# Beta's gate instructions at another place in a handwritten order of attention and GLU work

## The chip, the cores and the metric

The kernel runs on one core of one Trainium2 chip. The metric is device time in microseconds (us): how long the one core takes for one launch. The version before was timed three times: 264.73, 264.46 and 265.0 us, median 264.73 us.

## What is computed

Two branches read the same input `x` of 2048 tokens by 512 features, and a gate per token mixes them:

```
g = _sigmoid((x * gate_w).sum(-1, keepdims=True))
a = _A_ref(x, A_wq, A_wk, A_wv, A_wo, A_beta)
b = _B_ref(x, B_w_gate, B_w_up, B_w_down)
return g * a + (1 - g) * b
```

Branch B is a gated GLU: `gelu(x @ w_gate) * (x @ w_up)`, then `@ w_down`, with an inner width of 1792. Branch A is attention with 32 heads of width 16, in four segments of 512 tokens. In a segment the causal softmax attention `a_dot` is computed, and beside it a read `a_mem` from a running memory that the earlier segments filled; a gate per head, made from the 32 numbers of `beta`, mixes the two:

```
g = _sigmoid(beta).reshape(1, H, 1, 1)
...
o = g * a_mem + (1.0 - g) * a_dot
```

Everything here is about where the instructions stand that make the two factors `g` and `1 - g` of this last line.

## The kernel before

The work of all engines is cut into named tasks, each a short list of instructions for one engine. The string `ORDER` (lines 862 to 916) lists all tasks in one sequence, written out by hand. `schedule` (L134) reads it, and each engine receives its own tasks in that sequence and works through them strictly in order; `finalize` (L200) puts in the semaphore waits that the data need. A digit behind a task's name chooses one of four PSUM banks (psD, 128 x 512 in fp32) for a matmul task, and a letter chooses the engine of an eviction (`a` ScalarE, `d` VectorE, which the profile calls DVE). So a matmul task that gets a bank must wait until the task before it in that bank has been evicted.

Names in the order: `K0_1`, `Q1_2`, `V1_3b`, `G0_6` and `U0_7` are projections, the first number being the segment; K, Q, G and U tasks have four 128 x 512 matmuls (L449), V tasks four of 256 or 257 columns (L499). `Kev`, `Qev`, `Vev` and `Gev` evict them (L442 and L507 on ScalarE, L443 and L506 on DVE). `kpada` and `kpadb` (L488, DVE) write masked copies of K. `phk` and `phq` with `a`, `b` or `c` are the three steps of the feature map of the memory (L461 DVE, L463 ScalarE, L465 DVE). `st0_1B` computes a tile of attention scores in the four-bank buffer psX (L602), `exp0_1B` is its exponential on ScalarE (L609), `msk0_1B` multiplies its diagonal blocks by the causal mask on GpSimd (L615, called POOL in the profile). psX exists once, so `st`, `exp`, `st`, `exp` alternate. `pv0_1` (L644, 128 matmuls) multiplies the first two tiles' probabilities with V; it writes four banks in turn: 2 and 3 in its first half, 0 and 1 in its second half. `tp0_d01` and the three like it transpose its result on DVE (L530), and `pvp0_01` (L667 and L668) normalizes it and multiplies it by `gq`, the factor `1 - g`. That is the first attention tile that needs `gq`. The other factor, `gfull`, is first read in segment 1 (`ndp`, L558).

These tasks make the two factors, in `head_gates` (L761):

```
one("betab", DVE, 0.8, [I(lambda e, g=g: e.tensor_copy(
    betab[32 * g:32 * g + 32, :].rearrange("p (t j) -> p t j", j=2),
    ball[32 * g:32 * g + 32, :].rearrange("p (t g j) -> p g t j", g=4, j=2)[:, g]), ...
    for g in range(4)], bias=-150.0)
...
I(lambda e: e.activation(gq[:, :], betab[:], ACTF.Exp), ...
I(lambda e: e.activation(gfull[:, :], ball, ACTF.Exp, scale=-1.0), ...
```

`betab` (L764) is four copies on DVE, each of 32 partitions x 8 bf16, from `ball`, the 32 numbers of beta that the load `ld_beta` spread over all partitions of the buffer omem. `bexp` is two exponentials on ScalarE: L776 makes `gq` (128 x 8) and L777 `gfull` (128 x 32). `gqa` (L779, POOL) adds one to `gq`, `gqb` (L780, DVE) takes its reciprocal, `gfull` (L782, POOL) adds one to the other. No other task reads `betab`.

In the order before, `betab` stands on DVE behind `Vev1_0b` and ahead of `Gev0_1` and `kpada0_3`. `bexp` stands on ScalarE between `exp0_1A` (and the tiny `gr0`, L430) and `exp0_1B`. On POOL the sequence is `goa0 msk0_0A msk0_1A gqa msk0_1C msk0_1D gfull msk0_1B`. `gqb` stands on DVE behind `kpada1_0` and `gob0` (L434), ahead of `Qev1_3`.

Of the kernel before, what the change touches and what calls it, by code (L numbers as in the profile page):

```python
# [864 lines left out]
Kev0_3:a Q0_0:0 ld_wg0b Qev0_0:a Q0_1:3 st0_0A gwtr:2 Kev0_1:d gwev Q0_3:0 ld_wv ld_wg0 Qev0_1:d V0_1b:1 V0_3a:2 V0_3b:3 exp0_0A Qev0_3:d Vev0_3a:a  # L865
Vev0_1b:a st0_0B Vev0_3b:d kpada0_2 kpada0_1 V0_0b:0 V0_1a:2 V0_2a:1 Vev0_0b:d G0_6:3 Gev0_6:d Vev0_1a:d Vev0_2a:d exp0_0B st0_0C exp0_0C Q0_2:0
G0_2:3 V0_2b:2 ld_x1_2 ld_x1_1 ld_x1_3 ld_x1_0 ld_beta st0_0D Vev0_2b:a exp0_0D Gev0_2:d kpadb0_1 Qev0_2:d phka0_0 V1_2b:1 V0_0a:3 G1_6:2 V1_0b:0
Vev1_2b:d phka0_2 st0_0E Vev0_0a:d Vev1_0b:d betab G0_1:1 Gev1_6:a exp0_0E Gev0_1:d Q1_2:3 V1_3b:2 V1_3a:0 kpada0_3 Qev1_2:d Vev1_3a:d phkb0_2 phkc0_2
Vev1_3b:d st0_1A gz0 exp0_1A gr0 bexp Q1_0:1 V1_0a:3 G1_5:0 Vev1_0a:d Gev1_5:d st0_1B Q1_1:2 K1_0:3 exp0_1B phkb0_0 ld_wu1 ld_x2_0 G0_5:0 Qev1_0:d
kpadb0_3 vsh0_21 st0_1C exp0_1C Qev1_1:d ld_x2_1 ld_x2_3 ktr0_3 ld_wg1 Gev0_5:d V1_2a:1 K1_3:2 K1_1:0 vsh0_01 Vev1_2a:a vsh0_20 ld_x2_2 ktr0_2 vsh0_00  # L870
ld_wd1 st0_1D phkc0_0 Kev1_1:d kpada1_1 G0_4:1 G0_3:0 Gev0_4:d Kev1_0:d Gev0_3:d Kev1_3:a ld_wd0 ld_wu0 ktr0_1 ktr0_0 vsh1_20 ld_wo V1_1a:2 Vev1_1a:d
exp0_1D st0_2A exp0_2A msk0_0B msk0_0D msk0_0C kpada1_0 msk0_0E goa0 gob0 msk0_0A msk0_1A gqa gqb msk0_1C msk0_1D gfull msk0_1B G0_0:1 Q1_3:3 G1_1:0
Qev1_3:d phqa1_0 st0_2B Gev0_0:d Gev1_1:a pv0_1:2301 exp0_2B tp0_d01 tp0_d00 pvp0_01 Q2_0:3 Qev2_0:d tp0_d11 st0_2C K1_2:2 Kev1_2:d pvp0_00 tp0_d10
gelu0 G0_8:3 G0_13:1 gd0_13 G0_10:2 G0_11:0 G0_9:1 gd0_8 gd0_10 gd0_9 gd0_11 G0_12:3 G0_7:2 gd0_12 G1_2:1 U0_0:0 gd0_7 Gev1_2:d pvp0_11 h0_0 U0_13:3
U0_10:2 h0_10 Q2_1:1 Qev2_1:d exp0_2C st0_2D mz0:0 U0_7:2 U0_9:1 pvp0_10 h0_13 exp0_2D phqb1_0 st0_2E exp0_2E phka1_0 h0_7 mza0 h0_9 ota0_0 phqa1_2
kpadb1_0 G1_4:3 U0_1:2 h0_1 Gev1_4:a V1_1b:0 st0_3A G1_0:1 U0_5:3 Q2_2:2 exp0_3A Vev1_1b:a Gev1_0:a Qev2_2:a kpadb1_1 st0_3B exp0_3B U0_11:0 U0_4:1
U0_12:2 st0_3C phkb1_0 exp0_3C phqc1_0 kpada1_2 h0_4 h0_5 U0_6:1 U0_2:3 h0_11 h0_12 phqb1_2 h0_2 G1_3:0 Gev1_3:d h0_6 kpadb1_2 st0_3D phka1_2 U0_3:2
h0_3 U0_8:3 h0_8 Q2_3:0 Qev2_3:d exp0_3D phkb1_2 msk0_2A msk0_2B msk0_2C msk0_3A msk0_2E msk0_2D msk0_3C goc0 msk0_3B st1_0A msk0_3D pv0_3:1230
exp1_0A st1_0B exp1_0B tp0_d20 tp0_d21 pvp0_20 tp0_d30 ota0_1 pvp0_21 tp0_d31 kpada1_3 out0_1_0:1 out0_1_1 out0_1_2 V2_0a:2 Vev2_0a:d G1_9:3 V2_1b:0
Vev2_1b:d wev0_1:d st1_0C G1_8:2 G1_10:0 G1_11:1 gelu1 gd1_9 G1_7:3 gd1_8 gd1_10 gd1_7 gd1_11 G1_13:2 gd1_13 G1_12:0 gd1_12 phqc1_2 phkc1_0 mzq0  # L880
pvp0_31 pvp0_30 ota0_3 V2_0b:3 Vev2_0b:d ota0_2 V2_1a:1 Vev2_1a:d out0_0_0:2 out0_0_1 out0_0_2 nd1_0:0 ndp1_0 phkc1_2 exp1_0C st1_0D exp1_0D K2_0:3
# [63 lines left out]
```

## Time and profile before

| What | Value |
|---|---|
| median of three runs | 264.73 us |
| the profiled execution's own time | 265.0 us |
| its span, first to last instruction | 263.3 us |
| time outside the span, 265.0 - 263.3 | 1.7 us |
| granted TensorE clock, mean | 0.999 |
| busy: TensorE (PE) / DVE / ScalarE (ACT) / POOL | 258.8 / 199.5 / 203.2 / 98.5 us |
| `betab` L764 | 4 copies, 160 to 645 ns, from 22.6 to 24.6 us |
| `bexp` L776, L777 | 198 and 218 ns, at 27.3 and 27.4 us |
| `gqa` L779 and `gfull` L782 | 241 ns at 29.5 us and 337 ns at 37.7 us |
| `gqb` L780 | 168 ns at 37.9 us |

Times inside the profile count from the start of the span. A row of the timeline gives the start, the duration, the engine, the line and the operation, and in brackets how long the engine had been idle before it and what ended that. Rows of equal instructions that follow each other are merged; x4 says how many. Matmuls overlap: a 512-column matmul is shown as lasting 380 ns, while the next one starts about 216 ns after it. On DVE an instruction often starts 0.08 us before the one ahead of it has ended. In what follows such overlaps are kept as the rows show them.

### The profile page before, as it was taken

The numbers are of one execution on the slowest core, as the hardware profiler recorded it, in microseconds if no ns is written. First come the engines' busy times: TensorE is split into PE (matmuls) and PEld (weight loads), VectorE is DVE, ScalarE is ACT, GpSimd is POOL, SyncE is SP. The second block draws the span as 40 slices with busy tenths as digits, with TensorE's granted clock in tenths as the row PEclk, the third lists the DMA queues.
The fourth block names the chain that finished last, engine by engine and source line by source line (L and its number), as shares of the span: only waits on it lengthen the run. The fifth ranks groups of instructions, "written<-read, shape, count | busy, mean of one in ns | idle before, by whom it ended". The sixth has DMA issues, their size and how long they took to land.

```text
span 263.3 us, 6705 instructions
## 1 busy us (share of the span) xinstructions
PE 258.8 (98%) x2849; PEld 123.0 (47%) x2849; DVE 199.5 (76%) x412; ACT 203.2 (77%) x171; POOL 98.5 (37%) x163
## 2 busy tenths in 40 slices
PE   8999999999999999999999999999999999999995
PEld 7655445444354543544445445444444433444542
DVE  1559979284888686778958988976895973899873
ACT  1389779889988878898987898788788788777312
POOL 5008363024510465104806384156500377345300
PEclk9999999999999999999999999999999999999999
DMA  7974499400010211430002200022450000001412
GB/s 184 267 95 157 93 282 345 118 2 1 0 33 2 55 47 32 94 80 2 2 0 67 39 0 0 5 41 62 47 100 0 2 1 22 2 0 42 62 42 80
DMA packets 31990, 16.50 MB, mean 63 GB/s; under 512 B 21592, under 2 KB 31960, under 8 KB 31960
## 3 DMA queue, kind: packets, MB, share of 16 engines
q1 hardware_dynamic: 31272, 15.22, 25.6%
q10 hardware_dynamic: 688, 0.85, 0.9%
q8 instruction: 22, 0.36, 0.6%
q14 instruction: 8, 0.07, 0.1%
HBM read 7.87 MB, written 2.10 MB: 38 GB/s over the span
## 4 chain that ended last, share of the span: by engine, by line
PE 93%; DVE 4%; DMA 2%; issue 1%; SPq 0%; DVEq 0%
PE psD L449 46%; PE psD L735 19%; PE psX L602 9%; PE psD L644 6%; PE psD L749 5%; PE psD L499 4%; PE psD L477 2%; DMA wk<-in_A_wk_dram 2%; PE psD L547 1%; PE psD L577 1%; DVE betab L764 1%; DVE vnat L506 1%; DVE qT L443 0%; DVE phk L465 0%; DVE kD L488 0%
## 5 line engine op out<-in xcount | busy, mean ns | idle before, releaser
L609 ACT ACTIVATE pt<-psX 128x2048 bf16<-128x2048 f32 x72 | 135.1, 1877 | 29.0 <-PE psX L602 27.4
L615 POOL TENSOR_TENSOR pt<-pt,ctri 128x256 bf16<-128x256 bf16 x128 | 91.4, 724 | 129.8 <-ACT pt L609 125.4
L449 PE MATMUL psD<-xT,wu 128*128 128x512 bf16 x224 | 54.6, 380 | 0.0
L449 PE MATMUL psD<-xT,wg 128*128 128x512 bf16 x224 | 53.4, 380 | 0.0
L735 PE MATMUL psD<-wd,gb 128*128 128x512 bf16 x224 | 53.2, 380 | 0.0
L720 DVE TENSOR_TENSOR gb<-psD,gb 128x512 bf16<-128x512 f32 x56 | 37.2, 681 | 10.8 <-PE psD L449 10.8
L449 PEld LDWEIGHTS psD<-xT,wg 128*128 128x128 bf16 x224 | 20.9, 98 | 24.5 <-issue 1.3
L735 PEld LDWEIGHTS psD<-wd,gb 128*128 128x128 bf16 x224 | 20.7, 98 | 24.3 <-issue 2.1
L449 PEld LDWEIGHTS psD<-xT,wu 128*128 128x128 bf16 x224 | 20.2, 98 | 24.7 <-issue 2.6
L602 PE MATMUL psX<-qT,kD 32*128 32x192 bf16 (+7 forms) x512 | 28.6, 287 | 0.0
L530 DVE STREAM_TRANSPOSE tT<-psD 128x512 f32<-128x512 f32 x32 | 21.8, 702 | 5.1 <-PE psD L644 4.6
L443 DVE CAST gb<-psD 128x512 bf16<-128x512 f32 x20 | 13.6, 688 | 12.0 <-PE psD L449 11.9
L602 PEld LDWEIGHTS psX<-qT,kD 32*128 32x128 bf16 x512 | 8.2, 92 | 25.1 <-ACT pt L609 13.8
L499 PE MATMUL psD<-wv,xT 128*128 128x257 bf16 (+1 forms) x128 | 18.2, 273 | 0.3 <-DVE qT L443 0.3
L753 DVE SCALAR_TENSOR_TENSOR ost<-psD,gtok,wds 128x512 bf16<-128x512 f32 (+1 forms) x17 | 11.9, 711 | 7.7 <-PE psD L749 7.6
L668 DVE SCALAR_TENSOR_TENSOR ob<-tT,gq,rc 128x256 bf16<-128x256 f32 x32 | 16.7, 522 | 1.1
L703 ACT ACTIVATE gb<-psD 128x512 bf16<-128x512 f32 x28 | 15.0, 594 | 3.4 <-PE psD L449 3.3
L644 PE MATMUL psD<-pt,vsh 64*17 64x128 bf16 (+7 forms) x512 | 17.2, 283 | 0.0
L644 PE MATMUL psD<-pt,vnat 64*17 64x192 bf16 (+7 forms) x512 | 17.1, 283 | 0.0
L449 PE MATMUL psD<-xT,wq 128*128 128x512 bf16 x64 | 16.3, 380 | 0.1
L749 PE MATMUL psD<-wo,oT 128*128 128x512 bf16 (+1 forms) x68 | 16.1, 367 | 0.0
L499 PEld LDWEIGHTS psD<-wv,xT 128*128 128x128 bf16 x128 | 11.7, 97 | 7.2 <-issue 1.3
(81 smaller groups left out, 260.6 us busy)
## 6 DMA issues: line engine op xcount, KB each, us to landing
out_dram<-ost SPq DMA_DIRECT2D x15, 128.0 KB, 1.9
wu<-in_B_w_up_dram SPq DMA_DIRECT2D x2, 896.0 KB, 8.5
wd<-in_B_w_down_dram SPq DMA_DIRECT2D x2, 896.0 KB, 6.8
vsh<-vnat SPq DMA_DIRECT2D x16, 68.0 KB, 2.7
wg<-in_B_w_gate_dram SPq DMA_DIRECT2D x1, 896.0 KB, 5.5
wq<-in_A_wq_dram SPq DMA_DIRECT2D x2, 256.0 KB, 3.3
wv<-in_A_wv_dram SPq DMA_DIRECT2D x1, 512.0 KB, 4.2
wo<-in_A_wo_dram SPq DMA_DIRECT2D x1, 512.0 KB, 4.7
```

What stands on the lines that cost most here:

```text
L449: one(name, PE, n * T_MM, [I(lambda e, i=i: e.matmul(BK[sl.i][:, :], lhs(i), rhs(i), start=(i == 0), stop=(i == n - 1)), reads(i), [bk(sl) ...
L499: one(f"V{s}_{m}{'ab'[hf]}", PE, 2 * T_MM, [I(lambda e, i=i, sl=sl, a=a, z=z, xs=xs: e.matmul(BK[sl.i][:, 0:z - a], xs(i), wv[:, i, a:z], ...
L530: one(f"tp{name}", DVE, 0.605, [I(lambda e, sl=sl, ti=ti: e.transpose(tT[ti][:, :], BK[sl.i][:, :]), [bk(sl)], [("tT", ti)])], bias=bias)
L602: ins.append(I(lambda e, t=t, kb=kb, ncol=ncol, c0=c0, g=g: e.matmul(XALL[:, g * 512 + c0:g * 512 + c0 + ncol], kD[(4 * s + t) % R_KD][32 ...
L609: one(f"exp{s}_{name}", ACT, 2048 * 0.000833 + 0.05, [I(lambda e: e.activation(pt[slot][:, :, :], xin, ACTF.Exp, scale=ATT_SCALE), [("X",) ...
L615: ins.append(I(lambda e, mv=mv: e.tensor_tensor(mv, mv, cm, ALU.mult), [("pt", slot), ("causal",)], [("pt", slot)]))
L644: ins.append(I(lambda e, kb=kb, slot=slot, c0=c0, n=n, g=g, r0=r0, sl=banks[j], va=va: e.matmul(BK[sl.i][32 * g:32 * g + 17, 64 * kb:512], ...
L668: I(lambda e, ti=ti, ri=ri, t=t, j=j, dst=dst: e.scalar_tensor_tensor(out=dst, in0=t_rows(ti), scalar=gq[:, 2 * t + j:2 * t + j + 1], in1= ...
L703: t = one(f"gd{s}_{ft}", ACT, 0.485, [I(lambda e, gi=gi, f=f, sl=sl: e.activation(gb[gi][:, f, :], BK[sl.i][:, :], ACTF.Gelu_apprx_tanh), ...
L720: one(f"h{s}_{ft}", DVE, 0.605, [I(lambda e, sl=sl, gi=gi, f=f: e.tensor_tensor(gb[gi][:, f, :], BK[sl.i][:, :], gb[gi][:, f, :], ALU.mult ...
L735: mm.append(I(lambda e, fb=fb, gi=gi, f=f, q=q, sl=sl: e.matmul(BK[sl.i][:, :], gb[gi][:, f, q], wd[:, fb, :], start=(fb == 0), stop=(fb = ...
L749: one(f"wo{s}_{qt}{sfx}", PE, 4 * T_MM * w / 512, [I(lambda e, kb=kb, q=q, so=so, c=c, w=w: e.matmul(BK[so.i][:, 0:w], oT[:, kb, q], wo[:, ...
```

## The change

Only the order string changes; no instruction is added, removed or altered, and the sequences on PE and in the DMA queue of SyncE stay the same. Five moves, in the order's own words (the rest of the string is only wrapped differently):

```diff
-Vev1_2b:d phka0_2 st0_0E Vev0_0a:d Vev1_0b:d betab G0_1:1 Gev1_6:a
+Vev1_2b:d phka0_2 st0_0E Vev0_0a:d Vev1_0b:d G0_1:1 Gev1_6:a
...
-Vev1_3b:d st0_1A gz0 exp0_1A gr0 bexp Q1_0:1
+Vev1_3b:d st0_1A gz0 exp0_1A gr0 Q1_0:1
...
-ld_wd1 st0_1D phkc0_0 Kev1_1:d
+st0_1D phkc0_0 betab Kev1_1:d
...
-exp0_1D st0_2A exp0_2A msk0_0B ... gob0 msk0_0A msk0_1A gqa gqb msk0_1C msk0_1D gfull msk0_1B
+exp0_1D bexp st0_2A exp0_2A msk0_0B ... gob0 msk0_0A msk0_1A msk0_1C msk0_1D gqa gfull msk0_1B
...
-Qev1_3:d phqa1_0 st0_2B Gev0_0:d Gev1_1:a pv0_1:2301
+Qev1_3:d phqa1_0 st0_2B Gev0_0:d gqb Gev1_1:a pv0_1:2301
```

Engine by engine: on DVE, `betab` goes from ahead of `Gev0_1` to between `phkc0_0` and `Kev1_1`, past 14 instructions of evictions, `kpada0_3`, `kpadb0_3`, `phkc0_2` and `phkc0_0`; `gqb` goes from behind `gob0` to between `Gev0_0` and `tp0_d01`, past `Qev1_3`, `phqa1_0` and `Gev0_0`. On ScalarE, `bexp` goes from behind `gr0` to between `exp0_1D` and `exp0_2A`. On POOL, `gqa` goes from behind `msk0_1A` to behind `msk0_1D`, so that it now stands just ahead of `gfull` and `msk0_1B`.

More of the change, by code (lines that the diff above doesn't have):

```diff
@@ L867 @@
 G0_2:3 V0_2b:2 ld_x1_2 ld_x1_1 ld_x1_3 ld_x1_0 ld_beta st0_0D Vev0_2b:a exp0_0D Gev0_2:d kpadb0_1 Qev0_2:d phka0_0 V1_2b:1 V0_0a:3 G1_6:2 V1_0b:0
-Vev1_2b:d phka0_2 st0_0E Vev0_0a:d Vev1_0b:d betab G0_1:1 Gev1_6:a exp0_0E Gev0_1:d Q1_2:3 V1_3b:2 V1_3a:0 kpada0_3 Qev1_2:d Vev1_3a:d phkb0_2 phkc0_2
-Vev1_3b:d st0_1A gz0 exp0_1A gr0 bexp Q1_0:1 V1_0a:3 G1_5:0 Vev1_0a:d Gev1_5:d st0_1B Q1_1:2 K1_0:3 exp0_1B phkb0_0 ld_wu1 ld_x2_0 G0_5:0 Qev1_0:d
-kpadb0_3 vsh0_21 st0_1C exp0_1C Qev1_1:d ld_x2_1 ld_x2_3 ktr0_3 ld_wg1 Gev0_5:d V1_2a:1 K1_3:2 K1_1:0 vsh0_01 Vev1_2a:a vsh0_20 ld_x2_2 ktr0_2 vsh0_00
@@ L871 @@
[L871 to L878, printed above, removed]
+Vev1_2b:d phka0_2 st0_0E Vev0_0a:d Vev1_0b:d G0_1:1 Gev1_6:a exp0_0E Gev0_1:d Q1_2:3 V1_3b:2 V1_3a:0 kpada0_3 Qev1_2:d Vev1_3a:d phkb0_2 phkc0_2
@@ new lines @@
+Vev1_3b:d st0_1A gz0 exp0_1A gr0 Q1_0:1 V1_0a:3 G1_5:0 Vev1_0a:d Gev1_5:d st0_1B Q1_1:2 K1_0:3 exp0_1B phkb0_0 ld_wu1 ld_x2_0 G0_5:0 Qev1_0:d kpadb0_3
+vsh0_21 st0_1C exp0_1C Qev1_1:d ld_x2_1 ld_x2_3 ktr0_3 ld_wg1 Gev0_5:d V1_2a:1 K1_3:2 K1_1:0 vsh0_01 Vev1_2a:a vsh0_20 ld_x2_2 ktr0_2 vsh0_00 ld_wd1
+st0_1D phkc0_0 betab Kev1_1:d kpada1_1 G0_4:1 G0_3:0 Gev0_4:d Kev1_0:d Gev0_3:d Kev1_3:a ld_wd0 ld_wu0 ktr0_1 ktr0_0 vsh1_20 ld_wo V1_1a:2 Vev1_1a:d
+exp0_1D bexp st0_2A exp0_2A msk0_0B msk0_0D msk0_0C kpada1_0 msk0_0E goa0 gob0 msk0_0A msk0_1A msk0_1C msk0_1D gqa gfull msk0_1B G0_0:1 Q1_3:3 G1_1:0
@@ new lines @@
+Qev1_3:d phqa1_0 st0_2B Gev0_0:d gqb Gev1_1:a pv0_1:2301 exp0_2B tp0_d01 tp0_d00 pvp0_01 Q2_0:3 Qev2_0:d tp0_d11 st0_2C K1_2:2 Kev1_2:d pvp0_00
+tp0_d10 gelu0 G0_8:3 G0_13:1 gd0_13 G0_10:2 G0_11:0 G0_9:1 gd0_8 gd0_10 gd0_9 gd0_11 G0_12:3 G0_7:2 gd0_12 G1_2:1 U0_0:0 gd0_7 Gev1_2:d pvp0_11 h0_0
+U0_13:3 U0_10:2 h0_10 Q2_1:1 Qev2_1:d exp0_2C st0_2D mz0:0 U0_7:2 U0_9:1 pvp0_10 h0_13 exp0_2D phqb1_0 st0_2E exp0_2E phka1_0 h0_7 mza0 h0_9 ota0_0
+phqa1_2 kpadb1_0 G1_4:3 U0_1:2 h0_1 Gev1_4:a V1_1b:0 st0_3A G1_0:1 U0_5:3 Q2_2:2 exp0_3A Vev1_1b:a Gev1_0:a Qev2_2:a kpadb1_1 st0_3B exp0_3B U0_11:0
@@ L879 @@
+U0_4:1 U0_12:2 st0_3C phkb1_0 exp0_3C phqc1_0 kpada1_2 h0_4 h0_5 U0_6:1 U0_2:3 h0_11 h0_12 phqb1_2 h0_2 G1_3:0 Gev1_3:d h0_6 kpadb1_2 st0_3D phka1_2
+U0_3:2 h0_3 U0_8:3 h0_8 Q2_3:0 Qev2_3:d exp0_3D phkb1_2 msk0_2A msk0_2B msk0_2C msk0_3A msk0_2E msk0_2D msk0_3C goc0 msk0_3B st1_0A msk0_3D pv0_3:1230
 exp1_0A st1_0B exp1_0B tp0_d20 tp0_d21 pvp0_20 tp0_d30 ota0_1 pvp0_21 tp0_d31 kpada1_3 out0_1_0:1 out0_1_1 out0_1_2 V2_0a:2 Vev2_0a:d G1_9:3 V2_1b:0
```

## The prediction

> **What bounds the kernel.** I read the page first (busy times, chain), then the chain of waits in order of time, then the timeline of each engine around the moved instructions. The page's chain says that TensorE sets the end almost everywhere:
>
> ```profile
> PE 93%; DVE 4%; DMA 2%; issue 1%; SPq 0%; DVEq 0%
> ```
>
> So a saving counts only where PE waits. In the chain of waits (start, us, what) the 4% of DVE is one block:
>
> ```profile
> 22.64 0.06 DVE gzr L506
> 22.70 0.57 DVE betab L764
> ...
> 24.12 0.53 DVE betab L764
> ...
> 24.68 0.69 DVE gb L443
> ...
> 28.61 0.05 issue
> 28.66 2.76 PE psD L449 x12
> ...
> 39.98 2.19 PE psD L644 x108
> ...
> 72.62 2.08 PE psD L644 x126
> ```
>
> From 18.97 to 28.66 us the path runs through DVE, and `betab` is on it for 2.0 us. From 28.66 until 259.4 every piece is PE. The last two lines are for later: `pv0_1` takes 2.19 us, the same product in the next pair of tiles 2.08. Where PE really stood still is in its own timeline:
>
> ```profile
> 24.96 0.39 PE L602 MATMUL psX<-qT,kD 32*128 32x512 bf16 x4
> 25.42 1.04 PE L449 MATMUL psD<-xT,wq 128*128 128x512 bf16 x4
> 26.80 0.61 PE L499 MATMUL psD<-wv,xT 128*128 128x256 bf16 x4 [0.34 <-DVE qT L443]
> 27.25 1.02 PE L449 MATMUL psD<-xT,wg 128*128 128x512 bf16 x4
> 28.20 0.40 PE L602 MATMUL psX<-qT,kD 32*128 32x448 bf16 x8
> 28.66 1.04 PE L449 MATMUL psD<-xT,wq 128*128 128x512 bf16 x4
> ```
>
> These are `st0_1A`, `Q1_0`, `V1_0a`, `G1_5`, `st0_1B`, `Q1_1`. Without waits the steps from start to start are 0.33 for a score task (36.55 to 36.88), 0.86 for four 512-column matmuls (22.25 + 0.88 to 23.13, 23.13 to 23.99), 0.45 from a V task to a G task (as here, 26.80 to 27.25) and 0.95 from a G task to a score task (27.25 to 28.20). From 24.96 to 28.66 that is 0.33 + 0.86 + 0.45 + 0.95 + 0.33 = 2.92 us; it took 3.70. **PE lost 0.78 us here**, of `betab`'s 2.0.
>
> **Removing `betab` at 22.70.** I walk DVE again with its own rows. An eviction starts 0.03 us after the row of its matmuls ends. `Gev0_1`: its matmuls end at 22.25 + 1.04 = 23.29, so it runs 23.32 to 24.01 instead of 24.68 to 25.37. `kpada0_3`, at its present 0.74: to 24.78. `Qev1_2` to 25.38, `Vev1_3a` to 25.71, `phkc0_2` (1.21) to 26.84, `Vev1_3b` with its small copy to 27.23. PE, without waits: `Q1_0` 25.29 (its bank is free at 24.01), `V1_0a` 26.15 (bank free at 25.38), `G1_5` 26.60 (25.71), `st0_1B` 27.55, `Q1_1` 27.88 (27.23). `st0_1B` also needs psX, which `exp0_1A` frees at 25.41 + 1.88 = 27.29. Each is early by at least 0.2 us, so all of 28.66 - 27.88 = 0.78 is gained. `phkc0_2` would now start while POOL still masks (until 26.0, below); if that holds it up by 0.35 us, `Q1_1`'s bank is free at 27.6, still in time.
>
> After this, everything that depends on PE moves 0.78 forward together. What does not is DMA: the nearest landing is that of `vsh0_00` (issued at 34.95, landed at 38.24), 1.9 us before `pv0_1` reads it, so the shift fits in. The moved instructions issue no DMA themselves, and beta's own load, issued at 16.6 and landed 4.9 us later, is there long before either place.
>
> **Adding `betab` behind `phkc0_0`.** The places on DVE (two stretches):
>
> ```profile
> 32.07 1.22 DVE L465 SCALAR_TENSOR_TENSOR phk<-kT,phk 128x1024 bf16<-128x1024 bf16 x1
> 34.06 0.69 DVE L443 CAST kT<-psD 128x512 bf16<-128x512 f32 x1 [0.78 <-PE psD L449]
> ...
> 39.43 0.93 DVE L461 TENSOR_SCALAR phq<-qT 128x1024 bf16<-128x1024 bf16 x1
> 40.28 0.68 DVE L443 CAST gb<-psD 128x512 bf16<-128x512 f32 x1
> 41.17 1.31 DVE L530 STREAM_TRANSPOSE tT<-psD 128x512 f32<-128x512 f32 x2 [0.21 <-PE psD L644]
> ```
>
> DVE is idle for 0.78 us ahead of `Kev1_1`. How long are the copies there? Three of the four took 0.53 to 0.65 us and the third 0.16, at equal size. POOL tells why:
>
> ```profile
> 20.22 5.78 POOL L615 TENSOR_TENSOR pt<-pt,ctri 128x256 bf16<-128x256 bf16 x8
> ...
> 29.52 0.24 POOL L779 TENSOR_SCALAR gq<-gq 128x8 f32<-128x8 f32 x1
> 33.76 1.41 POOL L615 TENSOR_TENSOR pt<-pt,ctri 128x256 bf16<-128x256 bf16 x2 [4.00 <-ACT pt L609]
> ...
> 38.04 2.04 POOL L615 TENSOR_TENSOR pt<-pt,ctri 128x256 bf16<-128x256 bf16 x3
> ```
>
> At 22.7 POOL masked without a pause (to 26.0), and the long copies end near the ends of its instructions. Behind `phkc0_0` it is idle, for 4.00 us. Bounds for the four copies there: 4 x 0.16 + 3 x 0.03 = 0.73 us, and 4 x 0.645 + 0.09 = 2.67. I take 0.73, the row without POOL beside it. It fits into 0.78, price nothing. Behind `betab` stand `Kev1_1` and then `G0_3`, which wants that bank at 35.16 and has it at 34.75; so PE pays only for what exceeds 0.78 + 0.36 = 1.14.
>
> The Trainium skill (SBUF — State Buffer, "Who interferes with whom") says that DVE copies in some modes and all GpSimd work use one port pair, and whoever issues first holds it for the whole instruction. The trace agrees: 0.16 against 0.53 to 0.65 us. If the copies' 2.02 us were their own work instead, the sum would be that of the second rival below.
>
> **`bexp`, `gqb`, `gqa`.** At its old place `bexp` stood in 1.06 us of ACT idle time, so its removal gives nothing; at the new one ACT is idle for 0.72 us (36.28 to 37.00) and `bexp` took 0.31: nothing. `gqb` left 0.72 us of DVE idle time (nothing) and goes into the 0.21 ahead of `tp0_d01`; its instruction adds about 0.09 with the usual overlap, 0.17 without. Behind it a late `tp0_d01` would hold up `Q2_0`, which has 0.2 us. Nothing.
>
> `gqa` in front of `msk0_1B` moves POOL's row of 38.04 by 0.2 to 0.24 us. `pv0_1` reads that product 1.65 us after it is made: no loss. But DVE's `phqa1_0` (39.43) meets it. It took 0.93, against a median of 0.46 and a least of 0.39 for its line, and ended 0.28 after POOL's third mask of that row (40.08): it began just after that mask had begun. Behind it `Gev0_0` ended at 40.96, and `pv0_1` entered its second half, which writes that bank, at 41.01. That is the 2.19 against 2.08 us: **0.11 us of PE**. With POOL 0.2 later, `phqa1_0` finds the second mask still running, to about 39.67, and comes in ahead of the third; it ends near 39.95, `Gev0_0` near 40.55, and the second half (without waits at 40.90) does not wait. Bounds: +0.11, or, if it is behind the third mask again (40.32), it ends at 40.60 and `pv0_1` loses 0.24 more. I take +0.11, nearest to what the long copies of `betab` did: they got in between two masks.
>
> **Sum.** 0.78 + 0 + 0.11 = 0.89 us. Span 263.3 to 262.4; the execution's own 265.0 to 264.1. The median shown is 0.27 lower, 264.73 - 0.89 = 263.84, which I predict (0.34% faster).
>
> **Rivals.**
>
> A. The phase between `phqa1_0` and the masks goes the other way, or the 0.11 does not come: 0.78 - 0.24 = 0.54 to 0.78, 263.95 to 264.19. For it: `phqa1_0` lost its turn before, by 0.02 us. Against: it now asks some 0.2 us ahead of a mask's end. By the skill's section above (whoever issues first) a DVE instruction that waits already should come before the next mask; that is the forecast.
>
> B. The gain is returned: the copies keep 2.02 us. `Kev1_1` is then 1.28 late, `G0_3` some 0.85, and `betab` has only moved PE's wait: 0.89 - 0.85, 264.7, no change. For it: only one copy of four was ever short. Against: POOL's 4.00 us of idle time. A smaller return somewhere behind, where DVE is nearly full (41.2 to 46.6, PE's slack 0.2 to 0.3 us), also ends between.
>
> C. Slower. Same place, with all four copies as the longest: 2.67 us, 1.53 over the 1.14, so 0.89 - 1.53: 265.4. It decides from 1.14 + 0.89 = 2.03 us on for any loss (2.56 for one that can be measured), and needs POOL to mask all through `betab`; its next mask waits for `exp0_1C`, which ends after them. That the change does not do what it says is excluded: the instruction streams show these moves alone.
>
> **Chances and range.** Forecast (0.80 to 0.95 gained) 0.55; A 0.25; B with its partial returns 0.16; C 0.04. Range 263.5 to 264.5 us: down for the forecast plus the 0.27 between runs, up past A into the partial returns. What a measurement can tell from no change is about 0.2%, 0.53 us: faster 0.79 (forecast, and A, whose worse end lies just on it), same 0.17, slower 0.04.
>
> **What would show it.** Right: `Q1_1` starts near 27.9; the four copies take under 0.8 us in all, and `Kev1_1` starts when its matmuls end; `phqa1_0` takes under 0.6 and `pv0_1` 2.08; the chain is PE from 19 us on. Wrong: a DVE wait ahead of `Q1_1`, `G0_3` or `pv0_1`'s second half, or a new PE gap behind 43 us.

## The result and the profile after

| | before | after |
|---|---|---|
| median | 264.75 us (22 runs) | 263.79 us (22 runs) |
| profiled execution, own time / span | 265.0 / 263.3 us | 263.46 / 261.7 us |

The ratio of the times is 0.9965, 95% interval 0.9952 to 0.9978: the changed kernel is 0.93 us faster (0.58 to 1.27). Predicted were 0.89 us and 263.84. That the two differ by no more than 0.04 us says little, since the interval is 0.7 us wide; the trace is the closer test.

The spans differ by more, 1.6 us, and the trace tells what of that is the change's. TensorE (PE) has the same instructions in the same order in both, so the starts of its tasks can be subtracted one by one. `st0_1A`, ahead of which the change touches nothing that PE waits for, starts at 24.25 instead of 24.96: 0.71 us that come from the first loads, which land at other times in every run. Behind it:

| from start to start | before | after |
|---|---|---|
| `st0_1A` to `Q1_1` | 3.70 us | 2.93 us |
| `Q1_1` to `G0_3` | 6.50 | 6.50 |
| `G0_3` to `pv0_1` | 4.75 | 4.75 |
| `pv0_1` to `Q2_0` | 2.20 | 2.13 |
| `Q2_0` to the last matmul task | 217.59 | 217.58 |

The change therefore takes 0.77 + 0.07 = 0.84 us from PE's path, and nothing is given back in the 217 us that follow. I use these distances for the experiments too, since the first loads alone scatter the start of `st0_1A` between 24.16 and 24.96 us in these traces, as much as the effects looked for.

The page's chain of the changed kernel, by engine, has lost DVE's 4%:

```profile
PE 98%; DVE 0%; issue 0%; DVEq 0%
```

Its chain of waits in order of time (start, us, what), over the stretch where DVE and `betab` stood before, now names PE alone, and `pv0_1` has its 2.08 us:

```profile
24.31 0.33 PE psX L602 x4
24.64 0.97 PE psD L449 x4
25.61 0.44 PE psD L499 x4
26.05 0.86 PE psD L449 x4
26.91 0.33 PE psX L602 x8
27.24 2.70 PE psD L449 x12
...
38.48 2.08 PE psD L644 x128
```

PE's own timeline from `st0_1A` to `Q1_1` has no idle time left; the starts 24.25, 24.57, 25.45, 25.88, 26.84, 27.17 are 0.32, 0.88, 0.43, 0.96 and 0.33 apart, the prediction's unhindered steps to within 0.02:

```profile
24.25 0.39 PE L602 MATMUL psX<-qT,kD 32*128 32x512 bf16 x4
24.57 1.04 PE L449 MATMUL psD<-xT,wq 128*128 128x512 bf16 x4
25.45 0.60 PE L499 MATMUL psD<-wv,xT 128*128 128x256 bf16 x4
25.88 1.02 PE L449 MATMUL psD<-xT,wg 128*128 128x512 bf16 x4
26.84 0.40 PE L602 MATMUL psX<-qT,kD 32*128 32x448 bf16 x8
27.17 1.04 PE L449 MATMUL psD<-xT,wq 128*128 128x512 bf16 x4
```

On DVE `betab` lies where it was put, and it takes 0.73 us instead of 2.02. `Kev1_1` behind it starts 0.04 us after its matmuls end (32.53). Further on `phqa1_0` is down from 0.93 to 0.52:

```profile
30.58 1.22 DVE L465 SCALAR_TENSOR_TENSOR phk<-kT,phk 128x1024 bf16<-128x1024 bf16 x1
31.71 0.73 DVE L764 COPY betab<-omem 32x8 bf16<-32x8 bf16 x4
32.57 0.69 DVE L443 CAST kT<-psD 128x512 bf16<-128x512 f32 x1
...
37.94 0.52 DVE L461 TENSOR_SCALAR phq<-qT 128x1024 bf16<-128x1024 bf16 x1
```

POOL's timeline beside it: idle from 28.2, and the next mask at 32.27, in the same hundredth of a microsecond in which the last of the four copies starts:

```profile
26.94 1.29 POOL L615 TENSOR_TENSOR pt<-pt,ctri 128x256 bf16<-128x256 bf16 x2
32.27 1.45 POOL L615 TENSOR_TENSOR pt<-pt,ctri 128x256 bf16<-128x256 bf16 x2 [4.04 <-ACT pt L609]
...
36.76 2.22 POOL L615 TENSOR_TENSOR pt<-pt,ctri 128x256 bf16<-128x256 bf16 x3
```

### The profile page after: what moved, and what is told of

Same layout as the page of the kernel before. It is cut to its first block, busy times and chain, and to the rows that moved or that the text cites. A ratio compares the mean times of both kernels' runs of the same rounds, so it can differ in the third digit from the quotient of the medians.

```text
span 261.7 us, 6706 instructions
## 1 busy us (share of the span) xinstructions
PE 257.5 (98%) x2849; PEld 122.1 (47%) x2849; DVE 198.0 (76%) x412; ACT 203.2 (78%) x171; POOL 98.4 (38%) x163
## 4 chain that ended last, share of the span: by engine, by line
PE 98%; DVE 0%; issue 0%; DVEq 0%
PE psD L449 48%; PE psD L735 19%; PE psX L602 9%; PE psD L644 6%; PE psD L499 6%; PE psD L749 5%; PE psD L477 1%; PE psD L547 1%; PE psD L383 1%; PE psD L577 1%; DVE xT L795 0%; DVE ost L753 0%; PE psX L786 0%; DVEq L818 0%; PE psD L769 0%
## 5 line engine op out<-in xcount | busy, mean ns | idle before, releaser
L644 PE MATMUL psD<-pt,vsh 64*17 64x192 bf16 (+7 forms) x512 | 17.1, 283 | 0.0
```

The lines of the kernel that those rows point to most:

```text
L644: ins.append(I(lambda e, kb=kb, slot=slot, c0=c0, n=n, g=g, r0=r0, sl=banks[j], va=va: e.matmul(BK[sl.i][32 * g:32 * g + 17, 64 * kb:512], ...
```

## The experiments

The theory to be tested has two halves: `betab` cost PE 0.78 us only because POOL's masks beside it made the copies three to four times as long; and at the new place it is free because POOL is idle there and DVE has the room. Its rivals: the copies are that long of themselves, or the other moved instructions had a part in the gain, or the new place costs something that does not show.

**Which of the five moves counts.** `rest_alone` keeps `betab` at its old place and makes the other four moves.

```diff
-Vev1_0b:d G0_1:1
+Vev1_0b:d betab G0_1:1
...
-phkc0_0 betab Kev1_1:d
+phkc0_0 Kev1_1:d
```

> betab stays at its old place; bexp, gqa and gqb are moved as in the change. Theory: the 0.78 us are betab's alone, so st0_1A to Q1_1 stays at 3.70 us, and only the 0.06 us at pv0_1 are gained (from its start to that of Q2_0 2.14 us instead of 2.20); ratio 0.9998. Rival (bexp behind exp0_1A or gqb behind gob0 held something up too): the distance from st0_1A to Q1_1 or from there to pv0_1 shrinks, ratio 0.998 to 0.999.

Measured: ratio to before 0.9996 (0.9987 to 1.0006), 264.63 us. From `st0_1A` to `Q1_1` 3.70 us, from `pv0_1` to `Q2_0` 2.13. PE's timeline has the old hole, with the old cause:

```profile
24.99 1.04 PE L449 MATMUL psD<-xT,wq 128*128 128x512 bf16 x4
26.36 0.61 PE L499 MATMUL psD<-wv,xT 128*128 128x256 bf16 x4 [0.34 <-DVE qT L443]
```

So the 0.77 us are `betab`'s alone, and the 0.07 come from the other moves.

**Whether the new place is really free.** `no_betab` takes the four copies out of the changed kernel.

```diff
-I(lambda e: e.activation(gq[:, :], betab[:], ACTF.Exp), ...
+I(lambda e: e.activation(gq[:, :], ball[:, 0:8], ACTF.Exp), ...
...
-phkc0_0 betab Kev1_1:d
+phkc0_0 Kev1_1:d
```

> The changed kernel without betab's four copies; the first exponential reads eight of beta's numbers instead of each partition group's own, so the weights of the attention are not those of the reference. Theory: at the new place betab costs nothing, so this is as fast as the changed kernel, ratio to before 0.9965, PE without a wait in both. Rival (the new place costs something that the trace hides, in DVE's queue behind it): faster than the changed kernel by 0.2 us or more, ratio 0.9955 or below.

Measured: ratio 0.9971 (0.9956 to 0.9987), 263.68 us, and the distances of the changed kernel: 2.93, 6.50, 4.75, 2.13, 217.58. Without the copies nothing is faster than with them at the new place.

**Place or neighbour.** Now the two causes are crossed. First `betab` at its old place, with POOL idle; then at the new place, with POOL busy. The first pair of orders moves three mask tasks behind `msk0_1A`. The cut shows the kernel before, where they come behind `gqa` and `gqb` too; in the changed kernel, which has `gqa` and `gqb` elsewhere, the same three go right behind `msk0_1A`:

```diff
-msk0_0B msk0_0D msk0_0C kpada1_0 msk0_0E goa0 gob0 msk0_0A msk0_1A gqa gqb msk0_1C
+msk0_0B kpada1_0 goa0 gob0 msk0_0A msk0_1A gqa gqb msk0_0D msk0_0C msk0_0E msk0_1C
```

> The kernel before, with betab at its old place; on POOL three of the four first mask tasks (msk0_0D, C, E) go behind gqa, so that POOL is idle from 21.7 to 27.5 us while betab runs. Theory (the copies are short, and only POOL's masks beside them make them long): four copies 0.73 us in all instead of 2.02, kpada0_3 0.35 instead of 0.74, and PE's 0.78 us of waits between st0_1A and Q1_1 vanish although betab has not moved: 2.92 us from the start of the one to the start of the other instead of 3.70; ratio to before 0.997. Rival 1 (the copies have their length of themselves, or from ScalarE or DMA beside them): 2.0 us and 3.70 us as before, ratio 1.000. Rival 2 (place decides: anything ahead of Gev0_1 costs PE its whole length): 0.73 us still cost, a distance of 3.0 to 3.4 us.

> The changed kernel, with msk0_0D, C and E moved behind msk0_1A on POOL, so that POOL masks without a pause through betab's new place. Theory: the copies are long again, 2.0 to 2.7 us in all; Kev1_1 begins 1.2 to 1.9 us after its matmuls end; PE waits ahead of G0_3 for what exceeds 1.14 us, so 0.85 to 1.5 us; the gain is returned, ratio to before 0.999 to 1.003. Rival (the new place itself makes the copies short, whatever POOL does): 0.73 us, no wait ahead of G0_3, ratio 0.9965 as for the changed kernel.

Locally both went as the theory has it. At the old place the copies took 0.73 us, `kpada0_3` 0.35, and `st0_1A` to `Q1_1` was 2.93 us. At the new place they took 2.00 us, and `Q1_1` to `G0_3` rose from 6.50 to 7.60. But the whole times were 264.83 us (ratio 0.9994, 0.9971 to 1.0017) and 265.97 us (1.0046, 1.0031 to 1.0062): 0.7 and 0.9 us more than was expected of them. The distances show where: 1.2 and 0.9 us inside `pv2_3`, near 190 us, far from anything that was moved. The chain of waits of `old_place_masks_later` has it as "issue", time in which PE waited for nothing that the profile shows:

```profile
188.13 2.06 PE psD L644 x123
190.19 0.91 issue
191.10 0.29 PE psD L644 x5
```

In these two kernels the masks finish in another order than before, so `pv0_1` must wait for POOL at other points, and PE has 35 separate semaphore instructions instead of 36 (the one ahead of `pv0_1`'s second half is not there). The second pair gets the same idle and busy times of POOL without that: only `goa0` and `gqa` are pulled forward (`goa0`, which waits for ScalarE until 27 us, then holds up the masks behind it), the masks keep their order, and PE's and DVE's streams are unchanged.

```diff
-msk0_0B msk0_0D msk0_0C kpada1_0 msk0_0E goa0 gob0 msk0_0A msk0_1A gqa gqb msk0_1C
+msk0_0B goa0 gqa msk0_0D msk0_0C kpada1_0 msk0_0E gob0 gqb msk0_0A msk0_1A msk0_1C
```

> The kernel before, with betab at its old place, and on POOL goa0 and gqa pulled ahead of msk0_0D, C and E, so that POOL waits for ScalarE through betab; the masks keep their relative order, and with it PE's and DVE's instruction streams stay those of the kernel before. Theory (only POOL's masks make the copies long): betab 0.73 us, st0_1A to Q1_1 2.93 us instead of 3.70, nothing lost behind it, and the whole time gains what the change gains: ratio to before 0.997, without betab having moved. Rival (the 1.2 us that the first such order lost inside pv2_3 come from the masks' lateness itself): the same local gain, but PE loses about 1.2 us near 190 us again, ratio 1.000 or more.

Measured: ratio 0.9964 (0.9949 to 0.9978), 263.94 us. `betab` has not moved at all, and the whole gain is there. DVE's and POOL's timelines of this kernel:

```profile
22.28 0.73 DVE L764 COPY betab<-omem 32x8 bf16<-32x8 bf16 x4
23.04 0.69 DVE L443 CAST gb<-psD 128x512 bf16<-128x512 f32 x1
23.76 0.35 DVE L488 TENSOR_SCALAR kD<-kT,maskA 128x512 bf16<-128x512 bf16 x1
```

```profile
19.86 1.48 POOL L615 TENSOR_TENSOR pt<-pt,ctri 128x256 bf16<-128x256 bf16 x2
27.11 0.23 POOL L433 TENSOR_SCALAR gr<-gr 128x4 f32<-128x4 f32 x1 [5.77 <-ACT gq L776]
```

The copies stand in the same place of the same stream as before; the one thing that changed beside them is that POOL is idle from 21.3 to 27.1. And the opposite, the changed kernel with `goa0` pulled forward (its order has `gqa` and `gqb` elsewhere):

```diff
-msk0_0B msk0_0D msk0_0C kpada1_0 msk0_0E goa0 gob0 msk0_0A
+msk0_0B goa0 msk0_0D msk0_0C kpada1_0 msk0_0E gob0 msk0_0A
```

> The changed kernel with goa0 pulled ahead of msk0_0D, C and E on POOL in the same way, so that POOL masks without a pause through betab's new place; PE's and DVE's instruction streams stay those of the changed kernel. Theory: betab takes 2.0 us or more, PE waits 1.1 us ahead of G0_3 as in the first such order, nothing is lost near 190 us; the gain is returned and a little more: ratio to before 1.000 to 1.002. Rival (what is lost near 190 us comes from late masks): another 0.9 us there, ratio 1.004.

Measured: ratio 1.0011 (0.9999 to 1.0023), 265.13 us. Its DVE, POOL and PE timelines around the new place:

```profile
31.04 1.65 DVE L465 SCALAR_TENSOR_TENSOR phk<-kT,phk 128x1024 bf16<-128x1024 bf16 x1
32.61 2.08 DVE L764 COPY betab<-omem 32x8 bf16<-32x8 bf16 x4
34.72 0.69 DVE L443 CAST kT<-psD 128x512 bf16<-128x512 f32 x1
```

```profile
27.40 8.60 POOL L615 TENSOR_TENSOR pt<-pt,ctri 128x256 bf16<-128x256 bf16 x11
```

```profile
33.25 1.04 PE L449 MATMUL psD<-xT,wg 128*128 128x512 bf16 x4
35.47 1.04 PE L449 MATMUL psD<-xT,wg 128*128 128x512 bf16 x4 [1.18 <-DVE kT L443]
```

POOL masks through the whole stretch, three of the copies take 0.60 to 0.62 us and one 0.17, and PE waits ahead of `G0_3`: `Q1_1` to `G0_3` is 7.84 us, 1.34 more, and nothing is lost near 190 us. That is more than `betab`'s length alone would give: `phkc0_0` ahead of it is stretched as well, from 1.22 to 1.65. So the length of `betab` goes with POOL at either place, and the price at the new place is paid at `G0_3`, as the prediction said.

**The 0.07 us at `pv0_1`.** `one_gate_ahead` puts only `gqa` in front of `msk0_1B`, so that POOL's phase is about that of before.

```diff
-gqa gfull msk0_1B
+gqa msk0_1B
...
-msk0_2A msk0_2B
+msk0_2A gfull msk0_2B
```

> The changed kernel with gfull put behind msk0_2A on POOL, so that only one small gate operation, gqa, stands ahead of msk0_1B, as gfull alone did before. Theory (the phase between POOL's masks and phqa1_0 decides): phqa1_0 begins just after msk0_2A again and takes about 0.9 us, Gev0_0 is late, pv0_1 waits at its second half, 0.06 us more from pv0_1 to Q2_0 (2.20 instead of 2.13); ratio to the changed kernel 1.0002, to before 0.9967. Rival (the phase is not what made phqa1_0 slow): phqa1_0 0.5 us and 2.13 us as in the changed kernel.

Measured: ratio 0.9970 (0.9957 to 0.9983), 264.01 us. Half of it came: `phqa1_0` is long again,

```profile
38.64 0.82 DVE L461 TENSOR_SCALAR phq<-qT 128x1024 bf16<-128x1024 bf16 x1
39.39 0.68 DVE L443 CAST gb<-psD 128x512 bf16<-128x512 f32 x1
```

but `pv0_1` to `Q2_0` stayed at 2.13. `pv0_1` began at 39.12 and its second half 1.00 us later, at 40.12; `Gev0_0` ended at 40.06, just in time, where before it was late by some 0.1. The phase between the two engines makes `phqa1_0` long or short; whether PE pays depends on a tenth of a microsecond more.

It also depends on a second wait, which explains why 0.07 us were gained and not the whole 0.11. In the changed kernel the last matmul of `pv0_1` comes 0.12 us sooner after its first than before, but `Q2_0` comes only 0.07 sooner: it begins 0.25 us after that last matmul, while before, and behind the other seven products of this kind in both traces, it is 0.20. `Q2_0` writes bank 3, which the transpose `tp0_d01` must first have read, and PE's separate semaphore instruction ahead of `Q2_0` waits for DVE. That transpose follows the first half of `pv0_1`, so it did not move: it begins 1.27 us after `pv0_1`'s start (39.90 before, 38.41 after) in both kernels. Before:

```profile
41.17 0.72 DVE L530 STREAM_TRANSPOSE tT<-psD 128x512 f32<-128x512 f32 x1 [0.21 <-PE psD L644]
...
42.10 1.04 PE L449 MATMUL psD<-xT,wq 128*128 128x512 bf16 x4
```

After:

```profile
39.68 0.72 DVE L530 STREAM_TRANSPOSE tT<-psD 128x512 f32<-128x512 f32 x1 [0.52 <-PE psD L644]
...
40.55 1.02 PE L449 MATMUL psD<-xT,wq 128*128 128x512 bf16 x4
```

From the transpose's end to `Q2_0` it was 0.21 us before and is 0.15 now. The profile calls this wait "issue"; that it is the transpose is read from the banks, the semaphore and these times, and no run moved the transpose to test it.

`one_gate_ahead` also showed that the new place is not as safe as it looked. Its `betab` took 1.25 us: the last copy started together with `msk0_1C`, was held up by it and took 0.69 us. `G0_3` came 0.07 us late (6.57). `betab_behind_qev` puts the copies one gap earlier:

```diff
-phkc0_0 betab Kev1_1:d
+phkc0_0 Kev1_1:d
...
-Qev1_1:d ld_x2_1
+Qev1_1:d betab ld_x2_1
```

> The changed kernel with betab one gap earlier, between Qev1_1 and Gev0_5 on DVE: there DVE is idle for 0.77 us and POOL until 3 us later. In two of the kernels above betab at the changed kernel's place took 1.25 us, since its last copy met msk0_1C, and G0_3 came 0.07 us late. Theory (POOL beside the copies is all that matters): always 0.73 us here, G0_3 never late, Q1_1 to G0_3 6.50 us; ratio to before 0.9963 to 0.9970, no measurable difference to the changed kernel. Rival (DVE has no room here: phkc0_0 and Kev1_1 behind it become late): Q1_1 to G0_3 above 6.6 us.

Measured: ratio 0.9973 (0.9959 to 0.9987), 264.00 us; copies of 147 to 166 ns, 0.7 us in all, and `Q1_1` to `G0_3` as in the changed kernel. The trace is as expected. The ratio lies a little above the expected 0.9963 to 0.9970, which its interval covers, and the time cannot be told from the changed kernel's: no version here is measurably better than that one.

**What stopped PE near 190 us.** Two kernels change nothing but the number of warm-up matmuls on PE, which run while the first loads are under way.

```diff
-(("warm1", 45, 80), ...
+(("warm1", 44, 80), ...
```

> The changed kernel with 44 instead of 45 warm-up matmuls at the start of PE's program; nothing else. It tests why PE stood 1.2 and 0.9 us inside pv2_3 (near 190 us) in the two kernels with the masks behind gqa, which had one semaphore instruction less on PE. Theory (PE ran out of instructions there, because every instruction less shifts the place in the program at which the next block of it is loaded): a stall of 0.5 us or more inside pv2_3 here too, without any change to the masks; ratio to before about 1.000. Rival (the stall came from the masks' order): no stall, ratio 0.9965.

> The changed kernel with 46 instead of 45 warm-up matmuls on PE; nothing else. With one semaphore instruction or one warm-up matmul less on PE, the load of the next block of PE's program began 0.3 to 0.6 us after pv2_3's start instead of 1.8 us before it, and PE stood 0.9 to 1.2 us in pv2_3. Theory (the place in the program decides): two instructions more move the loads the other way, no stall inside pv2_3 or another one elsewhere, at a place where a block now ends badly; the load near 186 us begins ahead of pv2_3. Rival (any program other than these two lengths stalls there, or the stall goes with something else): 0.9 us inside pv2_3 again, ratio about 1.000.

Measured: with 44, ratio 0.9997 (0.9985 to 1.0009), 264.67 us, the whole gain gone again; with 46, 0.9962 (0.9946 to 0.9978), 263.88 us. In the kernel with 44, PE's timeline shows the hole in `pv2_3`, without any change to the masks:

```profile
189.31 0.35 PE L644 MATMUL psD<-pt,vnat 64*17 64x192 bf16 x8
190.30 0.28 PE L644 MATMUL psD<-pt,vsh 64*17 64x256 bf16 x4 [0.65 <-issue]
```

One of the DMA queues, which the profile calls "instruction", makes 22 transfers of 16 KB each. I take them for the loads of PE's program, because they move when that program gets longer or shorter. One of them begins 1.7 to 1.9 us before `pv2_3` in the kernels that do not stop there (before, after and six of the experiments; with 46 warm-ups 0.97 us before), and 0.29, 0.36 and 0.65 us after its start in the three that do. In all three PE stops 1.86 or 1.87 us into `pv2_3` and goes on 1.40 to 1.47 us after the end of this load. With 46 warm-ups the load ends as `pv2_3` starts, and 1.4 us later is still in time. So in these twelve traces the stop goes with this load, and the load's start with the length of the program: one or two instructions less put it behind the start of `pv2_3`. The rival, that late masks cause the stop, falls, since `one_warmup_less` has its masks where the changed kernel has them. Why so small a shift moves the load by 2 us, and what fills the 1.4 us between its end and PE's next instruction, stays open.

## Why the prediction was right, point by point

- **What bounds, and the 0.78 us.** Right: 0.77 measured, and `rest_alone` shows that they are `betab`'s alone. The walk's single times held too: `Gev0_1` starts 0.04 us after its matmuls, `phkc0_2` was held up by POOL as was allowed for (1.50 us instead of 1.21), and no bank was late.
- **`betab` at the new place: 0.73 us, price nothing.** Right in size to the hundredth, and `no_betab` shows the price. The reason given, POOL's idle time, is what the four crossed kernels show. One reading on the way was not right: the short copy at the old place did not run without POOL beside it. It began at 23.93 us, just before POOL's next mask at 23.95, and was not held up; the three long copies each ended 0.02 to 0.03 us after the end of a mask. The Trainium skill (SBUF — State Buffer, "Who interferes with whom": whoever issues first has the shared port pair for the whole instruction) agrees with the copies' lengths: 0.15 to 0.17 us alone, 0.53 to 0.69 where they wait for masks. That it is a port for which they wait, no run here shows.
- **The cover.** The prediction's figure was right where it was used, but its margin was argued too broadly: POOL's next mask was said to come after the copies. The prediction's own rows spoke against that: `exp0_1C`, for which this mask waits, ended at 33.68 us, and `phkc0_0`, behind which the copies were to stand, at 33.29, so that 0.73 us of copies would end at about 34.0. In the changed kernel the mask comes at the same moment as the last copy. In two experiments with `betab` at this place (`one_gate_ahead`, `one_warmup_less`) that copy was held up, which cost 0.07 us; in the changed kernel and in `one_warmup_more` it was not. So that the price was nothing, and not 0.07, was luck.
- **`bexp`, `gqa`, `gqb`: nothing.** Right; `gqb` took 0.18 us, and `tp0_d01` behind it still began on PE's release.
- **0.11 us at `pv0_1`.** The term that was mis-sized: 0.07 measured. `phqa1_0` came in between the masks as forecast, and the second half of `pv0_1` began without a wait, which shortened `pv0_1` by the 0.11. But the transpose `tp0_d01`, for which `Q2_0` behind it has to wait, did not come sooner. The step that was off is the room of 0.2 us that the prediction gave `Q2_0` there: it was 0.06 to 0.07, and that is all that could be gained. The sign that the prediction named, 2.08 us for `pv0_1` in the chain, came all the same: what `Q2_0` waits lies in the chain's next piece, which went from 0.97 to 1.01 us.
- **Rivals.** A was the nearest to what a run did: `one_gate_ahead` has its long `phqa1_0`, and still loses nothing there. But POOL's phase in it is that of the kernel before; A's own case, the phase shifted and lost, with its price of 0.24 us, did not come up in any run. The mechanism of B and C was right, and it sits where they said, ahead of `G0_3`; under full load it cost 1.34 us (`new_place_busy_pool`), between B's 0.85 and C's 1.53. B took the copies alone; `phkc0_0` grew with them.

## What to carry to other kernels

A small instruction on DVE has no fixed price: here the same four copies took 0.73 us with POOL idle and 2.0 with POOL masking, at either of two places. So before moving an instruction look at what the other engine does beside it; here moving POOL's work away gained as much as moving the copies. In a kernel that one engine bounds, subtract the starts of that engine's tasks between two traces: a gain and a loss elsewhere in the same run, which cancel in the total, then stand apart.

## What was not expected

By these traces PE can run out of instructions. `pv2_3` issues 128 matmuls with their weight loads in 1.88 us; when the load of the next 16 KB of program begins only after it has started, PE stops for about 0.9 to 1.2 us, until some 1.4 us after the load's end. Taking a single semaphore instruction or one warm-up matmul out of the program brought that about, 0.3 to 0.5% of the whole time, as much as the change under study gained. The Trainium skill (Runtime: NRT & Kernel Launch, "Instruction fetch mechanics") calls the crossing of a 16 KiB boundary mostly hidden; here one of the 22 loads was not hidden in three of the twelve traces, and whether it was hidden went with the program's length.
